# Pair 0 split from its two stacked q-k blocks, the weight clamp on GpSimd, and a contiguous tile for the middle 512 tokens

## The chip, the cores and the metric

The kernel runs on one core of a Trainium2 chip. The metric is the device time of one execution in microseconds. Before the change three runs gave 817.54, 816.72 and 815.52 us, so the median is 816.72 us. About 0.3% of that, 2.45 us, is what a measurement of this kernel can tell from no change.

## What is computed

Attention with hash buckets for 2 x 8 heads of 768 tokens and 64 dimensions, then two feed-forward blocks over the 1536 tokens of 512 values that it gives. Cut to what matters:

```python
q_bucket = sum(((q @ proj) > 0) * powers); k_bucket = sum(((k @ proj) > 0) * powers)
scores = where(q_bucket == k_bucket, (q @ k.T) / sqrt(64), -1e9)
attn = softmax(scores) @ v                      # -> x: 1536 x 512
xn = x / sqrt(mean(x * x) + 1e-6) * rms_g
y = silu(xn @ w_gate) * (xn @ w_val) @ w_out    # 512 -> 1536 -> 512
h = y @ moe2_w_in; g = where(h > 0, h, exp(min(h, 0)) - 1)
out = g @ moe2_w_out                            # 512 -> 2048 -> 512
```

The five weight matrices arrive as 64-bit floats and are turned into 32-bit ones on the chip.

## The kernel before

The work is written as some 2,700 tasks (`plan.add(engine, estimated us, function, reads, writes, ...)`) and the list `ORDER` says in which order their instructions are issued. There is no other scheduler: each engine takes its instructions in the order of that list and waits in front of the first one whose inputs or buffers aren't ready. All loads and stores go through SP's queue.

**Precision.** Every fp32 operand of a matmul is held as a high part rounded to `F32R` and a low part, the difference. A product is made of two or three passes (`PASS`: high x high, high x low, low x high).

**Attention.** Heads are worked in 8 pairs `j`, two heads `a` each. In memory `heads[2j+a]` holds three blocks of 128 x 768: `qk` (q in the upper 64 partitions, k in the lower), `kk` (k twice) and `qq` (q twice); `load_x` loads all three for both heads, six transfers of 384 KB. `prep` makes the operands: `ps_b` (bits of the buckets, from `qk`), `bitt`, `ps_c` (one-hot codes, with the table `wsel`, which `spread_table` copies from the loaded `wtmp`), and two operand tiles for each head, `tk` (`operand_k`, from `kk`: ScalarE the high part, GpSimd the low part) and `tq` (`operand_q`, from `qq`: GpSimd high and low, and a DMA `tq<-tq` that copies the high part to the lower partitions). For pair 0 these are done in two halves of 384 columns. Then come 12 score tiles a head pair: `ps_s` (4 matmuls), `nm` (row maximum, VectorE), `p` (exponential, ScalarE), transposes `ps_p`, their split into `pt` (ScalarE and VectorE, for some units ScalarE and GpSimd through `pf`), and `ps_v`. Two double banks hold `ps_s`, so the third score waits for the first exponential. `ps_w` are warm-up matmuls with no result.

**Weights.** `weights` loads a part of a matrix as `wraw`, takes the upper words' magnitude (`c1`, ScalarE, into `wf`), clamps it from below by `LEAST` (`c2`, VectorE, line 851), and puts sign, exponent and mantissa together with three integer operations (`c3`, `c4`, `c5`, VectorE, lines 857, 864, 871). ScalarE then rounds it to `whi` and GpSimd subtracts it to `wlo` (line 897). There are 54 such parts; six belong to the first feed-forward group and are done during attention. `wf` lives in the pool `h3` of 14 half-size tiles, as do the loaded head blocks.

**Feed-forward.** The first layer's 1536 inner columns are worked in five groups (3, 3, 2, 2, 2 tiles of 128), the second's in six. Group 0 takes the tokens in four blocks of 384, all later groups in three blocks of 512. A hidden tile `ps_h` is 12 matmuls (4 slices of 512 inputs, 3 passes). The inputs `xn` lie in one tile for each batch of 768 tokens, so the middle block of 512 tokens (512 to 1023) lies in two tiles, and `proj_mm` makes it in two parts of 256 columns, 24 matmuls.

The names that the change touches are `load_x` (312), `operand_k`, `operand_q`, `prep`, `score`, `weights` with its `c2`, `xsrc`, `xkeys`, `spread_table`, and `ORDER`.

Of the kernel before, what the change touches and what calls it, by code (L numbers as in the profile page):

```python
# [1278 lines left out]
```

## Time and profile before

| what | value |
|---|---|
| runs, us | 817.54, 816.72, 815.52 (median 816.72) |
| the profiled execution | 817.51 us |
| its span, first to last instruction | 815.4 us |
| mean granted TensorE clock | 0.996 of 2.4 GHz |
| busy, share of the span | PE 98%, VectorE 72%, ScalarE 50%, GpSimd 37% |

A matmul's end is modelled in these records, so a busy PE may still be waiting; the shares are means over stages with different limits. The program has a start of some 20 us, attention until about 250 us, the first feed-forward layer until about 565 us, and the second to the end.

### The profile page before, as it was taken

Reading aid. Unit: us, or ns where it says so; the run is one execution under the profiler, and the core shown is the slowest. Engines: PE = TensorE matmul, PEld = TensorE weight load, DVE = VectorE, ACT = ScalarE, POOL = GpSimd, SP = SyncE. Lnnn points to the kernel's source line nnn. Section 1 sums busy time; section 2 is a strip of 40 time slices with the busy share of each in tenths; the row PEclk is TensorE's granted clock in tenths of the full one; section 3 lists DMA queues with packets and bytes.
Section 4 is the critical chain, followed back from the end, with each engine's and each line's share of the span. In section 5 each row is a group of like instructions: output and inputs, shape, how many; then the busy total and the mean of one; then the engine's idle time right before and its main releaser. Section 6 shows DMA issues by size and latency. Waiting matters only on the chain.

```text
span 815.4 us, 11836 instructions
## 1 busy us (share of the span) xinstructions
PE 798.4 (98%) x4498; PEld 704.1 (86%) x4498; DVE 589.0 (72%) x914; ACT 411.0 (50%) x771; POOL 299.7 (37%) x255
## 2 busy tenths in 40 slices
PE   7999999989999999999999999999999999999998
PEld 6999798978999999988888888888888888888887
DVE  4898999999995873344546566878757777777676
ACT  4999898978995543322232232345544233432331
POOL 5889888879897020020111121111221021211110
PEclk8999999999999999999999999999999999999999
DMA  7638733551020023103012123122222201010004
GB/s 238 199 98 259 261 107 98 156 165 31 10 55 24 1 78 104 29 24 103 26 52 78 53 78 117 40 77 78 78 78 77 79 27 51 27 53 26 27 1 154
DMA packets 29592, 67.62 MB, mean 83 GB/s; under 512 B 3168, under 2 KB 3808, under 8 KB 29536
## 3 DMA queue, kind: packets, MB, share of 16 engines
q1 hardware_dynamic: 29536, 66.88, 26.4%
q8 instruction: 35, 0.57, 0.3%
q14 instruction: 21, 0.17, 0.1%
HBM read 57.82 MB, written 3.15 MB: 75 GB/s over the span
## 4 chain that ended last, share of the span: by engine, by line
PE 83%; DVE 9%; ACT 4%; issue 2%; DMA 1%; POOL 1%; SPq 0%; ACTq 0%; POOLq 0%
PE ps_h L946 40%; PE ps_o L1086 15%; PE ps_y L1031 12%; PE ps_s L514 5%; PE ps_p L559 5%; PE ps_v L606 4%; DVE nm L521 3%; DVE pt L571 2%; ACT p L531 1%; ACT pt L567 1%; DMA wtmp<-in_table_dram 1%; DMA vn<-in_v_dram 1%; PE ps_x L664 1%; DVE h L996 1%; DVE wf L851 0%
## 5 line engine op out<-in xcount | busy, mean ns | idle before, releaser
L897 POOL TENSOR_TENSOR wlo<-wf,whi 128x768 fp32r<-128x768 f32 (+1 forms) x54 | 92.4, 1724 | 446.1 <-ACT whi L893 379.3
L946 PE MATMUL ps_h<-xn,whi 128*128 128x256 f32 (+2 forms) x768 | 190.2, 336 | 0.0
L946 PEld LDWEIGHTS ps_h<-xn,whi 128*128 128x128 f32 x768 | 133.8, 189 | 11.9
L946 PE MATMUL ps_h<-xn,wlo 128*128 128x256 f32 (+2 forms) x384 | 128.9, 336 | 0.0
L992 ACT CAST h<-hf 128x512 fp32r<-128x512 f32 (+1 forms) x87 | 51.9, 606 | 134.2 <-DVE hf L986 47.0
L1086 PE MATMUL ps_o<-whi,h 128*128 128x512 f32 (+1 forms) x388 | 118.8, 387 | 0.4 <-DVE oa L1098 0.2
L946 PE MATMUL ps_h<-y,whi 128*128 128x512 f32 x384 | 118.2, 389 | 0.0
L521 DVE TENSOR_REDUCE nm<-ps_s 128x1 f32<-128x768 f32 x96 | 91.0, 948 | 6.1 <-PE ps_s L514 5.7
L606 PE MATMUL ps_v<-pt,vv 128*128 128x256 f32 x576 | 93.7, 292 | 0.6 <-DVE ot L624 0.2
L971 ACT ACTIVATE sg<-ps_h 128x512 f32<-128x512 f32 (+1 forms) x87 | 49.6, 580 | 87.4 <-PE ps_h L946 61.8
L514 PE MATMUL ps_s<-tk,tq 128*128 128x384 f32 x384 | 89.7, 356 | 2.9 <-ACT p L531 2.7
L1031 PE MATMUL ps_y<-h,whi 128*128 128x512 f32 (+1 forms) x312 | 91.7, 374 | 0.4 <-DVE h L996 0.4
L531 ACT ACTIVATE p<-ps_s,nm 128x768 f32<-128x768 f32 x96 | 87.2, 909 | 6.0 <-DVE nm L521 4.8
L559 PE MATMUL ps_p<-ident,p 128*128 128x128 f32 x576 | 84.3, 276 | 4.3 <-DVE pt L571 3.3
L1086 PEld LDWEIGHTS ps_o<-whi,h 128*128 128x128 f32 x388 | 72.6, 188 | 15.9 <-DVE oa L1098 0.7
L571 DVE TENSOR_TENSOR pt<-ps_p,pt 128x512 fp32r<-128x512 f32 x120 | 79.8, 681 | 8.7 <-ACT pt L567 7.6
L946 PEld LDWEIGHTS ps_h<-y,whi 128*128 128x128 f32 x384 | 72.1, 188 | 14.9
L996 DVE TENSOR_TENSOR h<-hf,h 128x512 fp32r<-128x512 f32 (+1 forms) x87 | 65.3, 762 | 23.9 <-ACT h L992 23.5
L606 PEld LDWEIGHTS ps_v<-pt,vv 128*128 128x128 f32 x576 | 78.7, 189 | 2.4 <-DVE pt L571 0.6
L946 PEld LDWEIGHTS ps_h<-xn,wlo 128*128 128x128 f32 x384 | 72.6, 189 | 5.7
L559 PEld LDWEIGHTS ps_p<-ident,p 128*128 128x128 f32 x576 | 67.4, 142 | 11.3 <-DVE pt L571 4.6
L567 ACT CAST pt<-ps_p 128x512 fp32r<-128x512 f32 x120 | 69.0, 587 | 12.8 <-PE ps_p L559 9.6
(89 smaller groups left out, 1287.2 us busy)
## 6 DMA issues: line engine op xcount, KB each, us to landing
wraw<-in_moe_w_out_dram SPq DMA_DIRECT2D x12, 768.0 KB, 4.5
qk<-in_heads_dram SPq DMA_DIRECT2D x16, 384.0 KB, 4.1
qq<-in_heads_dram SPq DMA_DIRECT2D x16, 384.0 KB, 4.0
kk<-in_heads_dram SPq DMA_DIRECT2D x16, 384.0 KB, 5.4
wraw<-in_moe_w_in_dram SPq DMA_DIRECT2D x8, 768.0 KB, 4.5
wraw<-in_moe_w_out_dram SPq DMA_DIRECT2D x10, 512.0 KB, 3.4
tq<-tq SPq DMA_DIRECT2D x21, 192.0 KB, 3.0
vn<-in_v_dram SPq DMA_DIRECT2D x8, 384.0 KB, 4.6
```

Source lines behind the costliest of these rows:

```text
L514: nc.tensor.matmul(st[B_][:, hf, 0:HS], lhsT=tq[:, x, c * 128:(c + 1) * 128], rhs=tk[:, x, hf * HS:(hf + 1) * HS], start=(x == 0), stop=(x ...
L521: nc.vector.tensor_reduce(out=st["nm", u, cc], in_=st[B_][:, :, 0:HS], axis=AX.XY, op=ALU.max, negate=True,)
L531: nc.scalar.activation(out=halves(st["p", u][:, cc]), in_=st.pop(B_)[:, :, 0:HS], func=AF.Exp, bias=st["nm", u, cc], scale=1.0, accum_out= ...
L559: nc.tensor.transpose(out=st[B_][:, o:o + 128], in_=p[:, cc, (2 * n + kt) * 128:(2 * n + kt + 1) * 128], identity=ident,)
L567: nc.scalar.copy(out=st[T_][:, 0], in_=st[B_])
L571: nc.vector.tensor_tensor(out=pt[:, 1], in0=st.pop(B_), in1=f(pt[:, 0]), op=ALU.subtract)
L606: nc.tensor.matmul(st[B_][:, 0:256], lhsT=st["vv", j][:, a, 2 * n + kt, :], rhs=pt[:, x, kt * 256:(kt + 1) * 256], start=(n == seq[0] and ...
L897: nc.gpsimd.tensor_tensor(out=l, in0=s["w"], in1=f(h), op=ALU.subtract)
L946: nc.tensor.matmul(ps[:, o:o + ln], lhsT=w[wp][:, kk, ft * 128:(ft + 1) * 128], rhs=t[xp][:, s:s + ln], start=(kk == 0 and n == 0), stop=( ...
L996: nc.vector.tensor_tensor(out=h[:, 1, 0:bw], in0=s["hf"], in1=f(h[:, 0, 0:bw]), op=ALU.subtract)
L1031: nc.tensor.matmul(s["ps"][:, 0:bw], lhsT=wo[wp][:, ft, m * 128:(m + 1) * 128], rhs=h[:, xp, 0:bw], start=(ft == 0 and i == 0), stop=(ft = ...
L1086: nc.tensor.matmul(s["ps"], lhsT=h[:, xp, t * 128:(t + 1) * 128], rhs=wo[wp][:, ft, ds], start=(ft == 0 and i == 0), stop=(ft == n - 1 and ...
```

## The change

Pair 0 loads only its two `qk` blocks. A new function, `first`, makes all its operands from them: ScalarE writes k and the scaled k into the two halves of `tk`, VectorE the low part of k and two scaled copies of q, GpSimd the high and the low part of q. The DMA `tq<-tq` is gone for pair 0, and the loads of pair 1 no longer wait for pair 0's first score. `spread_table` moves from VectorE to ScalarE. The clamp `c2` moves from VectorE to GpSimd, with a second bound that changes no weight. Sixteen new GpSimd copies (`middle`) put the middle 512 tokens into eight tiles of `h3`; `xsrc` hands these to groups 1 to 4 of the first layer. The list `ORDER` is a new one throughout. The estimates of `dma` differ, which by themselves issue nothing.

```diff
 def load_x(j, prio):
+        parts = ((0, 0), (0, 1)) if j == 0 else ((0, 0), (0, 1), (1, 0), (2, 0), (1, 1), (2, 1))
+        for n, (x, a) in enumerate(parts):
             dma(
-                lambda x=x, a=a: go(a, x), S * 128 * 4, r=[("go", j - 1)],
+                lambda x=x, a=a: go(a, x), S * 128 * 4, r=[("go", j - 1)] if j > 1 else [],
...
+    def first(a, prio):
...
+        def khi8():
+            nc.scalar.activation(out=operand(0, a, 1)[up, 0], in_=src()[dn], func=AF.Copy, scale=QSCALE)
+        def khi():
+            nc.scalar.copy(out=operand(0, a, 1)[dn, 0], in_=src()[dn])
+        def klo():
+            t = operand(0, a, 1)
+            nc.vector.tensor_tensor(out=t[dn, 1], in0=src()[dn], in1=f(t[dn, 0]), op=ALU.subtract)
+        def qhi8(x):
+            nc.vector.tensor_scalar(
+                out=operand(0, a, 0)[dn, x], in0=src()[up], scalar1=QSCALE, scalar2=None, op0=ALU.mult
+            )
+        def qhi():
+            nc.gpsimd.tensor_copy(out=operand(0, a, 0)[up, 0], in_=src()[up])
+        def qlo():
+            t = operand(0, a, 0)[up, 0]
+            nc.gpsimd.tensor_tensor(out=t, in0=src()[up], in1=f(t), op=ALU.subtract)
...
             def c2():
-                nc.vector.tensor_scalar(
-                    out=s["w"], in0=s["w"], scalar1=LEAST, scalar2=None, op0=ALU.max
+                nc.gpsimd.tensor_scalar(
+                    out=s["w"], in0=s["w"], scalar1=MOST, scalar2=LEAST, op0=ALU.min, op1=ALU.max
                 )
...
     def xsrc(g, blk, kk):
+        if li == 0 and g and blk == 1:
+            return [(0, st["mid", kk], 0, bw)]
...
+    def middle(prio):
+        def copy(kk, p, b):
+            if ("mid", kk) not in st:
+                st["mid", kk] = [half([128, 512], F32R, "mid") for _ in range(2)]
+            nc.gpsimd.tensor_copy(
+                out=st["mid", kk][p][:, b * 256:(b + 1) * 256],
+                in_=st["xn", b, kk][:, p, (1 - b) * 512:(1 - b) * 512 + 256],
+            )
...
     def spread_table():
-            nc.vector.tensor_copy(out=wsel[rows, hf], in_=st["wtmp"][rows])
+            nc.scalar.copy(out=wsel[rows, hf], in_=st["wtmp"][rows])
```

What the new list does at the places that the prediction speaks of:

SP's queue at the program's start, before (`qk`, `qq`, `kk`: head blocks; `pj`: the hash projection; `wtmp`: the table; `vn`: v):

```order
L321 DMA qk<-in_heads_dram 128x768
L1142 DMA pj<-in_proj_dram 128x32
L321 DMA qk<-in_heads_dram 128x768
L321 DMA qq<-in_heads_dram 128x768
L321 DMA kk<-in_heads_dram 128x768
L1135 DMA wtmp<-in_table_dram 128x256
L321 DMA kk<-in_heads_dram 128x768
L405 DMA tq<-tq 64x384
L332 DMA vn<-in_v_dram 128x768
```

SP's queue there, after:

```order
L322 DMA qk<-in_heads_dram 128x768 x2
L1207 DMA pj<-in_proj_dram 128x32
L1200 DMA wtmp<-in_table_dram 128x256
L322 DMA qk<-in_heads_dram 128x768 x2
L334 DMA vn<-in_v_dram 128x768
L322 DMA qq<-in_heads_dram 128x768
```

The table has two head blocks ahead of it in place of four, and what follows it are loads of pair 1 and v.

TensorE at the start, before:

```order
L1148 MATMUL ps_w<-ident 128x128 x11
L424 MATMUL ps_b<-qk,pj 32x384 x4
L1148 MATMUL ps_w<-ident 128x128 x5
L443 MATMUL ps_c<-bitt_82,wsel 128x384 x4
L514 MATMUL ps_s<-tk,tq 128x384 x12
L559 MATMUL ps_p<-ident,p 128x128 x4
L514 MATMUL ps_s<-tk,tq 128x384 x4
```

TensorE at the start, after:

```order
L1213 MATMUL ps_w<-ident 128x128 x10
L465 MATMUL ps_b<-qk,pj 32x384 x4
L1213 MATMUL ps_w<-ident 128x128 x3
L484 MATMUL ps_c<-bitt_82,wsel 128x384 x3
L1213 MATMUL ps_w<-ident 128x128 x3
L484 MATMUL ps_c<-bitt_82,wsel 128x384
L557 MATMUL ps_s<-tk,tq 128x384 x8
L465 MATMUL ps_b<-qk,pj 32x384 x4
L557 MATMUL ps_s<-tk,tq 128x384 x4
```

Three warm-up matmuls now stand between the third and the fourth `ps_c`, and pair 1's `ps_b` stands ahead of the third score.

VectorE at the first weight part (`wf_1077`), in pair 2, before:

```order
L624 TENSOR_TENSOR ot_1218<-ps_v_1129,ot_1218 64x256
L851 TENSOR_SCALAR wf_1077<-wf_1077 128x768
L521 TENSOR_REDUCE nm_1260<-ps_s_1220 128x1
L857 TENSOR_SCALAR wf_1077<-wf_1077 128x768
L571 TENSOR_TENSOR pt_1270<-ps_p_1225,pt_1270 128x512
L521 TENSOR_REDUCE nm_1285<-ps_s_1251 128x1
```

VectorE there, after (the part is `wf_1050`):

```order
L564 TENSOR_REDUCE nm_1217<-ps_s_1165 128x1
L900 TENSOR_SCALAR wf_1050<-wf_1050 128x768
L716 TENSOR_TENSOR xT_1163<-ot_763,ps_x_1204 128x384
L564 TENSOR_REDUCE nm_1240<-ps_s_1208 128x1
L667 TENSOR_TENSOR ot_1238<-ps_v_1113,ot_1238 64x256
L614 TENSOR_TENSOR pt_1247<-ps_p_1225,pt_1247 128x512
```

GpSimd there, after:

```order
L383 TENSOR_TENSOR tk_1034<-kk_886,tk_1034 64x768
L342 CAST vv_1072<-vn_955 128x6x64
L348 TENSOR_TENSOR vv_1072<-vn_955,vv_1072 128x6x64
L894 TENSOR_SCALAR wf_1050<-wf_1050 128x768
L623 CAST pt_1128<-pf_1090 128x512
L348 TENSOR_TENSOR vv_774<-vn_672,vv_774 128x6x64
```

The clamp has left VectorE's row and stands in GpSimd's between an operation on v and the cast of a transposed tile; VectorE's first operation on that part is now `c3` (line 900), which waits for it.

## Rows read from the trace of the kernel before

**Rows 1.** The page: busy time by engine, and the chain by engine.

```profile
PE 798.4 (98%) x4498; PEld 704.1 (86%) x4498; DVE 589.0 (72%) x914; ACT 411.0 (50%) x771; POOL 299.7 (37%) x255
...
PE 83%; DVE 9%; ACT 4%; issue 2%; DMA 1%; POOL 1%; SPq 0%; ACTq 0%; POOLq 0%
```

**Rows 2.** Windows: stretch, length, busy PE, PEld, DVE, ACT, POOL, clock, DMA share, GB/s.

```profile
12.00:20.00 8.00, 7.06 (x27) 6.07 (x26) 5.63 (x8) 5.98 (x13) 7.65 (x12) 0.57 0.82 280
20.00:80.00 60.00, 60.00 (x460) 56.82 (x458) 53.07 (x82) 58.24 (x120) 53.16 (x53) 1.00 0.61 184
80.00:160.00 80.00, 76.20 (x572) 71.05 (x570) 78.64 (x116) 72.72 (x146) 66.31 (x57) 1.00 0.54 164
160.00:240.00 80.00, 75.73 (x545) 68.37 (x544) 77.57 (x118) 69.34 (x143) 68.33 (x62) 1.00 0.21 57
```

**Rows 3.** Chain that ended last, the program's start: start us, us, what.

```profile
3.04 6.43 DMA wtmp<-in_table_dram
...
10.20 1.06 DVE wsel L1157
...
11.31 0.46 PE ps_c L443
...
12.78 0.68 PE ps_s L514 x2
...
14.48 1.00 ACT p L531 x2
...
20.57 0.78 PE ps_b L424 x8
21.35 0.90 PE ps_s L514 x4
```

**Rows 4.** DMA issues of the first microseconds: KB, us to landing.

```profile
qk<-in_heads_dram SPq DMA_DIRECT2D x1, 384.0 KB, 3.1
...
qq<-in_heads_dram SPq DMA_DIRECT2D x1, 384.0 KB, 6.1
```

**Rows 5.** Timeline of the start: start us, us, engine, line, operation.

```profile
0.72 0.38 SPq L321 DMA_DIRECT2D qk<-in_heads_dram  x1
...
7.12 1.38 PE L1148 MATMUL ps_w<-ident 128*128 128x128 f32 x10
```

**Rows 6.** Windows of TensorE alone: stretch, length, busy, clock, DMA share, GB/s.

```profile
13.00:17.00 4.00, 3.21 (x11) 0.52 0.73 235
```

**Rows 7.** Groups by shape: count, busy us, mean ns, idle before.

```profile
L851 DVE TENSOR_SCALAR wf<-wf 128x768 f32<-128x768 f32 x28 | 20.8, 747 | 8.3 <-ACT wf L848 8.3
...
L897 POOL TENSOR_TENSOR wlo<-wf,whi 128x768 fp32r<-128x768 f32 x28 | 55.7, 2003 | 245.5 <-ACT whi L893 212.4 <-PE ps_h L946 18.6 <-PE ps_o L1086 14.6
...
L409 POOL TENSOR_TENSOR tq<-qq,tq 64x768 fp32r<-64x768 f32 x14 | 26.8, 1917 | 0.5
...
L398 POOL TENSOR_SCALAR tq<-qq,share 128x768 fp32r<-128x768 f32 x14 | 14.2, 1012 | 2.0 <-DMA qq<-in_heads_dram 1.8
...
L893 ACT CAST whi<-wf 128x768 fp32r<-128x768 f32 x28 | 23.4, 839 | 12.4 <-DVE wf L871 12.4
```

**Rows 8.** The clamp, line 851: its durations until 260 us; VectorE's time from 80 to 245.

```profile
L851 DVE TENSOR_SCALAR wf<-wf x6: 544/1240/1545, 84.1 to 195.4; 128x768 f32<-128x768 f32 x6
...
80.00:245.00 165.00, 6.57 (x6) 1.00 0.38 112
```

**Rows 9.** Chain in the first layer: one middle and one outer hidden tile.

```profile
405.31 2.87 PE ps_h L946 x24
...
412.29 2.72 PE ps_h L946 x12
```

**Rows 10.** Chain in both layers: the longest pieces that aren't TensorE's.

```profile
503.36 2.70 DVE h L996 x2
...
673.90 1.51 DVE sg L980
...
767.37 1.66 DVE wf L851 x2
```

More of the change, by code (lines that the diff above doesn't have):

```diff
@@ L18 @@
 LEAST = 2.0 ** -15
+MOST = 3.4028234663852886e38
 SLOTS, H3S, PTS = 22, 14, 4
@@ L311, in dma @@
     def dma(fn, nbytes, r=(), w=(), prio=None):
-        return plan.add("SP", max(0.57, nbytes / 360e3), fn, r, w, prio, 2.7)
+        return plan.add("SP", max(0.5, nbytes / 315e3), fn, r, w, prio, 2.3)
     st = {}
@@ L321, in go @@
             nc.sync.dma_start(out=st["x", j, a, x], in_=heads[2 * j + a, x])
-        for n, (x, a) in enumerate(((0, 0), (0, 1), (1, 0), (2, 0), (1, 1), (2, 1))):
+        parts = ((0, 0), (0, 1)) if j == 0 else ((0, 0), (0, 1), (1, 0), (2, 0), (1, 1), (2, 1))
+        for n, (x, a) in enumerate(parts):
             dma(
-                lambda x=x, a=a: go(a, x), S * 128 * 4, r=[("go", j - 1)],
+                lambda x=x, a=a: go(a, x), S * 128 * 4, r=[("go", j - 1)] if j > 1 else [],
                 w=[("h3", "x", j, a, x)], prio=prio + 0.05 * n,
@@ L414, in operand_q, with src, key @@
         plan.add("Pool", pool(n), lo, [X_], los, prio)
+    def first(a, prio):
+        X_ = ("h3", "x", 0, a, 0)
+        def src():
+            return st["x", 0, a, 0]
+        def key(i, *parts):
+            return [okey(0, a, i, (x, h)) for x in parts for h in range(2)]
+        def khi8():
[14 more added lines that the diff above has]
+            nc.gpsimd.tensor_tensor(out=t, in0=src()[up], in1=f(t), op=ALU.subtract)
+        plan.add("ACT", act(S) + 0.12, khi, [X_], key(1, "hi"), prio)
+        plan.add("DVE", dve(S), klo, [X_, *key(1, "hi")], key(1, "lo"), prio)
+        plan.add("ACT", act(S) + 0.25, khi8, [X_], key(1, "up"), prio)
+        for x, part in enumerate(("hi", "dup")):
+            plan.add("DVE", 0.065 + S / 1920.0 + 0.2, lambda x=x: qhi8(x), [X_], key(0, part), prio)
+        plan.add("Pool", 0.83, qhi, [X_], key(0, "lo"), prio)
+        plan.add("Pool", pool(S), qlo, [X_], key(0, "lo"), prio)
     def prep_bits(j, prio):
@@ L491, in prep @@
         for a in range(2):
-            for cols in ((0,), (1,)) if j == 0 else ((0, 1),):
-                operand_k(j, a, cols, prio + off("opk", j) + a * off("opa", j))
-                operand_q(j, a, cols, prio + off("opq", j) + a * off("opa", j))
+            if j == 0:
+                first(a, prio + a)
+            else:
+                operand_k(j, a, (0, 1), prio + off("opk", j) + a * off("opa", j))
+                operand_q(j, a, (0, 1), prio + off("opq", j) + a * off("opa", j))
     def unit(u):
@@ L537, in score @@
         need = [okey(j, a, 0, (p, c // 3)) for p in ("hi", "lo", "dup", "hot")]
-        need += [okey(j, a, 1, (p, hf)) for hf in range(2) for p in ("hi", "lo", "hot")]
+        need += [okey(j, a, 1, (p, hf)) for hf in range(2) for p in ("hi", "lo", "hot", "up")]
         plan.add("PE", 4 * mm(HS) + 0.04, pe, need, w, prio + off("S", j))
@@ L877, in weights @@
             slow = 1.0
-            plan.add("DVE", slow * (0.065 + cols / 1920.0), c2, [], [W_], prio)
+            plan.add("Pool", 0.12 + cols * 0.00105, c2, [], [W_], prio)
             plan.add("DVE", slow * (0.065 + cols / 1920.0), c3, [], [W_], prio)
@@ L926, in xkeys @@
             return [(("slot", "y2", kk, p), x) for kk in range(KD) for p in range(2) for x in units(g, blk)]
+        if g and blk == 1:
+            return [(("h3", "mid", kk, p), b) for kk in range(KD) for p in range(2) for b in range(B)]
         keys = []
@@ L950, in proj_mm @@
             )
+    def middle(prio):
[6 more added lines that the diff above has]
+            )
+        for b in range(B):
+            for kk in range(KD):
+                for p in range(2):
+                    plan.add(
+                        "Pool", 0.36, lambda kk=kk, p=p, b=b: copy(kk, p, b),
+                        [(("slot", "xn", b, kk), p, 1 - b)],
+                        [(("h3", "mid", kk, p), b)] + ([(("h3", "mid", kk, 1), "got")] if p == 0 else []), prio,
+                    )
     def wkeys(g, m):
@@ L1156, in spread_table @@
             rows = slice(64 * hf, 64 * hf + 64)
-            nc.vector.tensor_copy(out=wsel[rows, hf], in_=st["wtmp"][rows])
-    plan.add("DVE", 0.55, spread_table, [("h3", "wtmp"), "wzero"], ["wsel"], -28)
+            nc.scalar.copy(out=wsel[rows, hf], in_=st["wtmp"][rows])
+    plan.add("ACT", 0.75, spread_table, [("h3", "wtmp"), "wzero"], ["wsel"], -28)
     load_v(0, -27)
@@ L1194 @@
     pos = float(NU)
+    middle(pos + 8)
     prev = None
```

276 rows, old and new, of the table ORDER are left out of this document.

## The prediction

> **What bounds the kernel now.** I read the page's busy shares and chain first, then windows by stage, then the chain of the start, and at last the groups by shape. TensorE is busy for 98% of the span and makes 83% of the chain; VectorE makes 9% [rows 1]. The windows say where these 9% lie. From 20 to 80 us TensorE is busy for all of 60.00 us, so what is gained ahead of 20 us is passed on. From 80 to 240 us it shows 151.9 of 160 us, while VectorE is busy for 156.2 of 160 us: there VectorE sets the pace, and TensorE lacks at least 8.1 us, more where a busy matmul is a waiting one [rows 2]. From about 240 us TensorE runs without a gap but for three places [rows 10]. Ahead of 20 us the chain is that of loading the table `wtmp`, which lands at 3.04 + 6.43 = 9.47 us, of copying it into `wsel` until 11.26, and of `ps_c` at 11.31; the first exponential starts at 14.48 and the fifth score at 21.35 [rows 3]. TensorE's granted clock was 0.52 of full speed, its lower level, from 13 to 17 us [rows 6], after it had stood from the end of the warm-up at 8.50 to 11.31 us [rows 3, 5].
>
> **The start.** Removed: four 384 KB loads of pair 0, its four `tq<-tq` copies, and the table's place behind four head blocks. SP's first issue is at 0.72 us [rows 5], the table's, the sixth, at 3.04 [rows 3], so issues are 0.46 us apart; as the fourth the table is issued at about 2.1. The first block took 3.1 us to land, the third 6.1 [rows 4]. So the table lands between 5.2 and 8.2; it has two blocks ahead of it and is a third of a block, and I take 6.6. The first `qk` lands at 3.8. From there three engines work side by side. ScalarE: the two high parts of k, by its cast of 768 columns 0.84 each [rows 7], until 5.5, then the table: the trace has no such copy on ScalarE; on VectorE the second took 1.06 [rows 3], as the upper bound for each, the lower is a third of a 768-column cast, 0.28; I take 0.4, nearer the cast, which is ScalarE's own, so `wsel` is ready at 6.6 + 0.8 = 7.4 (6.1 to 10.3). GpSimd: the high and the low part of q, 1.01 and 1.92 [rows 7], until 6.7. VectorE: two scaled copies of q, between the shortest and the longest clamp of that width, 0.54 and 1.55 [rows 8], the low part of k and the bits; these are ready between 7.4 and 8.7. So `ps_c` starts at 7.6 to 8.7, against 11.31: 2.6 to 3.7 us earlier. The three warm-up matmuls behind it cost 6 x 0.138 = 0.83 [rows 5], beside the one-hot copies that the score needs anyway. With 3.2 us the first exponential starts at 11.3. From there to the fifth score it was 6.87 us [rows 3]. Pair 1's `ps_b`, 0.78 [rows 3], now fills a wait: 0.8 less. If the clock stays up since TensorE no longer stands for 2.8 us, that stretch shrinks by up to two more microseconds; I don't count on it. **Sum 4.0 us**, bounds 1 (the table as late as 10) and 6. ScalarE, with 58.24 of 60 us busy from 20 to 80 [rows 2], is next in line there; its work behind the first exponential is not longer than before.
>
> **The clamp during attention.** Six clamps took VectorE 6.57 us between 80 and 245 us, 0.54 to 1.55 each [rows 8]. All of that stretch is VectorE's, so the gain has 6.6 us as its upper bound. The lower: a clamp of 1.2 us is one of 0.54 that waited, and where GpSimd was the cause, `c3`, now first, waits in its place; then 6 x 0.54 = 3.3 are left, and if TensorE finds something else to wait for, nothing. GpSimd's price for the two-bound form isn't in the trace; the nearest row is `tq<-qq,share`, two operations with immediate or column operands over 128x768: 1.01 [rows 7]; the upper bound is its subtraction, 1.92 to 2.00 [rows 7]. Six of these add 6 to 12 us to the 134.6 us that GpSimd works from 80 to 240 [rows 2]; it has 25 idle. `c3` waits for GpSimd on VectorE, and behind it in that row stand a maximum, a join and a subtraction for which ScalarE and TensorE wait; the order leaves one or more of GpSimd's operations between. **Sum 3.5 us**, bounds -2 and 6.6.
>
> **The middle tile.** A middle hidden tile of 24 matmuls takes 2.87 us, an outer one of 12 takes 2.72 [rows 9]. Groups 1 to 4 have 9 column tiles, each for gate and value: 18 x 0.15 = **2.7 us**, in a stage where TensorE never waits. The sixteen copies of 256 columns cost GpSimd about a third of 1.01 each, 5.4 us in all, in a stage where it stands idle for hundreds of microseconds ahead of `wlo` [rows 7]; they are needed only at group 1's second block. Were that cover gone, the price is 5.4 us once. The Trainium skill, "TensorE: Matmul & The Clock Gate", section "Back-to-back issue gap", gives a lone matmul N / 2.4 + 2.5 ns at full clock; by that 216 matmuls fewer would save an estimated 0.5 us. The rows give 0.15 us for 12 matmuls, 12.5 ns each; I go by them.
>
> **The clamp in the feed-forward layers.** 48 clamps leave VectorE, which gains nothing where TensorE sets the pace, but for the two that made a piece of 1.66 us of the chain [rows 10]. The same 48 add to GpSimd some 22 x 1.01 and 26 x 0.7 (that form scaled to 512 columns), 40 us. Two other pieces, 2.70 for two subtractions and 1.51 for one operation [rows 10], are VectorE's stretched; more GpSimd work makes more of these. I set the gain against the loss: **0**, bounds -3 and +1.7. Eight of the 14 tiles of `h3` go to the middle tokens through the first layer; 48 parts in some 550 us need one or two at a time, so six are enough, at no cost.
>
> **Sum.** 4.0 + 3.5 + 2.7 + 0 = 10.2 us. The profiled execution took 817.51 us (its span 815.4 and 2.1 around it), so 807.3; the median of the runs stands 0.8 below the profiled one, so I forecast **806.5 us**.
>
> **Rivals.** (1) *VectorE's time goes to other waits.* For it: the clamps' spread, 0.54 to 1.55 [rows 8], shows that VectorE's operations are held up by something beside them, and GpSimd gets busier. The attention term falls to 0 and the feed-forward stage loses 1: 811.0. The Trainium skill, "SBUF — State Buffer", section "Who interferes with whom", says that VectorE and GpSimd share a port pair which one of them holds for a whole instruction while the other is blocked; it speaks for this rival, and the clamps' spread agrees with it. (2) *Slower: the clamp as a wait in order.* `c3` heads VectorE's row until GpSimd has done the clamp, which may itself stand behind a `wlo` of 2.00 us [rows 7]; VectorE's sums and subtractions, which free TensorE's banks, stand behind it. It decides from 10.2 / 48 = 0.21 us of TensorE's time for each feed-forward part; at 0.3 us the time is 806.5 + 14.4 = 821. For it: one stretched operation of 1.5 us did reach TensorE. Against it: 54 `wlo`s ran beside VectorE, and three places in over 500 us lost anything [rows 10]. (3) *The table is late again*, 6.4 us after its issue as before, with ScalarE's copies at 1.06: the start gives 1 in place of 4: 809.5. For it: every transfer behind the first took 6 us or more until 10 us [rows 3, 4]. Against it: fewer bytes ahead. (4) *All terms at their good ends*, the clock staying up: 6 + 6.6 + 2.7 + 0 = 15.3: 801.4. (5) *The 0.15 us belong to that place and not to the number of matmuls*: the middle term falls to 0, 809.2; the other middle tiles of the chain with the same 2.87 us speak against it [rows 9]. The skill's formula above speaks for it. That the change doesn't do what it says can't be for the matmuls, whose order has none of 256 columns left in `ps_h`.
>
> **How the numbers follow.** Forecast 0.50, (1) 0.16, (2) 0.05, (3) 0.12, (4) 0.15, (5) 0.02. A measurement of this kernel can tell about 0.3%, 2.45 us, from no change. Faster by more than that: all but (2) and those parts of (1) and (3) where both go wrong together, 0.07: 0.88. Within: 0.07. Slower: 0.05. The range: (2), and the 0.07 near no change, are left out above, and some 0.06 of (4) below: 801 to 812.5.
>
> **What would show it.** Right: `ps_c` at 8 us or so and the first exponential at about 11; the first layer's middle hidden tiles at 2.72 us as the others; VectorE still nearly full from 76 to 235 us but without line 851; the first feed-forward matmul some 7 us earlier than before; about 1 us for a clamp on GpSimd. Wrong: `ps_c` at 10 or later; a clamp of 2 us on GpSimd; VectorE waiting for GpSimd ahead of `c3`; more than the three old places on the chain behind 270 us. The forecast fails as a whole if the new order makes attention's units meet in another way than before, with waits of TensorE between 20 and 80 us, where there were none.

## The result, and the profile after

The changed kernel took 808.41 us (median of four runs, 807.17 to 809.12), against 816.22 us for the kernel before beside it: a ratio of 0.990, 95% interval 0.988 to 0.992. It is faster by some 8 us; forecast were 806.5 us and 801 to 812.5. Measured again later, beside the variants, it took 807.18 us against 815.89 (ratio 0.988, 0.9865 to 0.990). The profiled execution took 808.29 us with a span of 806.5, which is 8.9 us less than before, where the sum had 10.2; the second measurement (e5) has a span of 805.5, 9.9 us less.

The page of the changed kernel, busy time and chain, answers to [rows 1]: VectorE has lost 13 us of work, GpSimd gained 48, and VectorE's share of the chain has not shrunk.

```profile
PE 793.1 (98%) x4282; PEld 690.9 (86%) x4282; DVE 576.0 (71%) x864; ACT 414.8 (51%) x776; POOL 347.4 (43%) x317
...
PE 82%; DVE 11%; ACT 2%; issue 2%; POOL 1%; DMA 1%; ACTq 0%; SPq 0%; DVEq 0%; POOLq 0%
```

The windows of [rows 2] (stretch, length, busy PE, PEld, DVE, ACT, POOL, clock, DMA share, GB/s):

```profile
12.00:20.00 8.00, 7.25 (x51) 5.79 (x50) 7.81 (x11) 7.38 (x16) 4.94 (x6) 1.00 0.27 76
20.00:80.00 60.00, 59.76 (x453) 57.20 (x454) 53.97 (x82) 57.52 (x118) 52.77 (x54) 1.00 0.57 183
80.00:160.00 80.00, 79.14 (x596) 73.55 (x595) 77.68 (x120) 74.93 (x153) 73.49 (x64) 1.00 0.47 148
160.00:240.00 80.00, 75.96 (x531) 69.36 (x530) 75.82 (x110) 68.52 (x140) 68.43 (x64) 0.98 0.25 70
```

From 12 to 20 us VectorE is now the full engine (7.81 of 8 us, before 5.63) and the clock stays at its upper level (1.00, before 0.57). From 80 to 160 us TensorE is busy for 79.14 us (before 76.20). From 160 to 240 us little is won.

The chain at the start (start us, us, what), beside [rows 3], is no longer that of the table: from 3.86 us to 22.15 it is VectorE's alone:

```profile
3.86 1.65 DVE tq L438 x2
...
5.86 2.14 DVE tk L435
...
8.03 0.63 DVE bitt L471
...
8.79 0.60 PE ps_c L484 x2
...
10.01 0.61 DVE tq L438
...
18.66 1.29 DVE tk L435
```

In the timeline of the same stretch (start us, us, engine, line, operation) stand the table's two copies, the first exponential and the fifth score:

```profile
6.06 0.82 ACT L1222 CAST wsel<-wtmp 64x256 fp32r<-64x256 f32 x2 [0.50 <-DMA wtmp<-in_table_dram]
...
12.55 0.90 ACT L574 ACTIVATE p<-ps_s,nm 128x768 f32<-128x768 f32 x1 [0.82 <-DVE nm L564]
...
16.66 0.97 PE L557 MATMUL ps_s<-tk,tq 128*128 128x384 f32 x4
```

The table is ready at 6.88, but the bucket bits only at 8.66, because VectorE's low part of k (line 435) took 2.14 us. The first exponential is 1.9 us earlier than before, the fifth score 4.7.

How much of this reaches TensorE is read from the number of its matmuls started by 70 us. Before (scores `ps_s`, products with v `ps_v`, one-hot codes `ps_c`; stretch, length, busy us, count, clock, DMA share, GB/s):

```profile
0.00:70.00 70.00, 26.44 (x108) 0.95 0.61 192
0.00:70.00 70.00, 21.09 (x128) 0.95 0.61 192
0.00:70.00 70.00, 4.02 (x12) 0.95 0.61 192
```

The same three after:

```profile
0.00:70.00 70.00, 26.44 (x116) 1.00 0.52 169
0.00:70.00 70.00, 22.43 (x136) 1.00 0.52 169
0.00:70.00 70.00, 4.86 (x15) 1.00 0.52 169
```

and what they cost in the chain of the changed kernel:

```profile
192.69 0.47 PE ps_v L649 x4
193.16 0.18 PE ps_c L484
...
195.52 0.70 PE ps_s L557 x4
```

Transposes stand at 144 in both. So at 70 us the changed kernel is ahead by 8 x 0.175 + 8 x 0.118 + 3 x 0.18 = 2.9 us: that is the start's worth, where the sum had 4.0. The same count gives 3.1 in e5 (116, 138, 15) and 2.4 in e9 (114, 136, 14), whose code is the same up to there. And some of it may be the clock of the one execution it is read against: before's profile has a mean granted clock of 0.996, with 0.57 from 12 to 20 us [rows 2]. Of the 41 executions of before beside the variants, the 13 with a mean clock of 1.000 took 815.4 us in the mean, the 18 with 0.997 or less 817.0; where in the program the clock fell in these, no trace shows.

The rest is in one table, from the first matmul of `ps_h`, the first of `ps_o` and the end of the span; attention, the first and the second layer are three lengths that add up to it, each read from the one execution that was profiled. The variants are those of the next section; e1 to e8 ran on one chip, e9 to e11 on a second, e12 on a third, so ratios, each to before beside it, compare better than medians.

| kernel | median us | ratio to before, 95% | attention ends | first layer | second layer |
|---|---|---|---|---|---|
| before | 816.22 | | 241.7 | 324.5 | 249.2 |
| changed | 808.41 | 0.988 to 0.992 | 235.6 | 321.3 | 249.6 |
| changed, again (e5) | 807.18 | 0.9865 to 0.990 | 234.1 | 321.4 | 250.0 |
| e1 middle in two | 808.51 | 0.989 to 0.992 | 234.3 | 324.3 | 249.4 |
| e2 clamp on VectorE | 814.30 | 0.9965 to 0.998 | 242.0 | 321.3 | 249.9 |
| e3 clamp on GpSimd in attention alone | 807.09 | 0.986 to 0.991 | 233.0 | 321.3 | 250.0 |
| e4 no clamp | 807.69 | 0.987 to 0.991 | 234.4 | 321.4 | 249.5 |
| e6 before, clamp on GpSimd | 811.77 | 0.993 to 0.996 | 237.4 | 324.2 | 248.6 |
| e7 no low q of head 0 | 807.21 | 0.987 to 0.9905 | 233.4 | 321.4 | 249.6 |
| e8 low k early | 807.43 | 0.987 to 0.991 | 234.5 | 321.4 | 249.4 |
| e9 join moved | 805.28 | 0.985 to 0.988 | 232.4 | 321.4 | 249.8 |
| e10 four loads back | 808.33 | 0.987 to 0.992 | 237.0 | 321.3 | 250.0 |
| e11 low q on VectorE | 804.53 | 0.984 to 0.988 | 234.8 | 321.3 | 249.5 |
| e12 e9 and e11 | 804.37 | 0.984 to 0.987 | 232.6 | 321.3 | 249.6 |

The layers repeat within some 0.6 us from program to program with the tile; attention scatters by 1 to 3 us between executions of code that is the same up to there (the changed kernel, e1, e3 and e5: 233.0 to 235.6). A difference of 1 us in a median is therefore read in its stage or not at all.

### The profile page after: what moved, and what is told of

Its sections match the earlier page's. It is cut to its first block, busy times and chain, and to the rows that moved or that the text cites. A ratio compares the mean times of both kernels' runs of the same rounds, so it can differ in the third digit from the quotient of the medians.

```text
span 806.5 us, 11405 instructions
## 1 busy us (share of the span) xinstructions
PE 793.1 (98%) x4282; PEld 690.9 (86%) x4282; DVE 576.0 (71%) x864; ACT 414.8 (51%) x776; POOL 347.4 (43%) x317
## 3 DMA queue, kind: packets, MB, share of 16 engines
q1 hardware_dynamic: 28640, 64.91, 25.3%
## 4 chain that ended last, share of the span: by engine, by line
PE 82%; DVE 11%; ACT 2%; issue 2%; POOL 1%; DMA 1%; ACTq 0%; SPq 0%; DVEq 0%; POOLq 0%
PE ps_h L993 38%; PE ps_o L1151 16%; PE ps_y L1096 12%; PE ps_v L649 5%; PE ps_p L602 5%; PE ps_s L557 4%; DVE nm L564 3%; DVE pt L614 2%; DVE wf L907 1%; DVE h L1061 1%; ACT p L574 1%; ACT pt L610 1%; DVE wf L914 1%; PE ps_c L484 1%; DVE wf L900 1%
## 5 line engine op out<-in xcount | busy, mean ns | idle before, releaser
L940 POOL TENSOR_TENSOR wlo<-wf,whi 128x768 fp32r<-128x768 f32 (+1 forms) x54 | 90.7, 1687 | 187.8 <-ACT whi L936 171.7
L993 PE MATMUL ps_h<-xn,whi 128*128 128x512 f32 (+1 forms) x480 | 138.3, 369 | 0.0
L894 POOL TENSOR_SCALAR wf<-wf 128x768 f32<-128x768 f32 (+1 forms) x54 | 45.5, 848 | 198.7 <-ACT wf L891 198.2
L993 PEld LDWEIGHTS ps_h<-xn,whi 128*128 128x128 f32 x480 | 88.4, 188 | 11.7
L1061 DVE TENSOR_TENSOR h<-hf,h 128x512 fp32r<-128x512 f32 (+1 forms) x87 | 68.7, 806 | 34.9 <-ACT h L1057 34.7
L557 PE MATMUL ps_s<-tk,tq 128*128 128x384 f32 x384 | 87.9, 350 | 1.5 <-ACT p L574 1.0
L993 PE MATMUL ps_h<-xn,wlo 128*128 128x512 f32 (+1 forms) x240 | 88.2, 367 | 0.0
L602 PE MATMUL ps_p<-ident,p 128*128 128x128 f32 x576 | 82.5, 276 | 1.9 <-DVE pt L614 0.8
L1151 PE MATMUL ps_o<-wlo,h 128*128 128x512 f32 (+1 forms) x194 | 75.1, 387 | 0.0
L993 PE MATMUL ps_h<-y,wlo 128*128 128x512 f32 x192 | 74.7, 389 | 0.0
```

What stands on the lines that cost most here:

```text
L557: nc.tensor.matmul(st[B_][:, hf, 0:HS], lhsT=tq[:, x, c * 128:(c + 1) * 128], rhs=tk[:, x, hf * HS:(hf + 1) * HS], start=(x == 0), stop=(x ...
L602: nc.tensor.transpose(out=st[B_][:, o:o + 128], in_=p[:, cc, (2 * n + kt) * 128:(2 * n + kt + 1) * 128], identity=ident,)
L940: nc.gpsimd.tensor_tensor(out=l, in0=s["w"], in1=f(h), op=ALU.subtract)
L993: nc.tensor.matmul(ps[:, o:o + ln], lhsT=w[wp][:, kk, ft * 128:(ft + 1) * 128], rhs=t[xp][:, s:s + ln], start=(kk == 0 and n == 0), stop=( ...
L1061: nc.vector.tensor_tensor(out=h[:, 1, 0:bw], in0=s["hf"], in1=f(h[:, 0, 0:bw]), op=ALU.subtract)
L1151: nc.tensor.matmul(s["ps"], lhsT=h[:, xp, t * 128:(t + 1) * 128], rhs=wo[wp][:, ft, ds], start=(ft == 0 and i == 0), stop=(ft == n - 1 and ...
```

## The experiments

**The middle tile undone (e1).**

```diff
     def xsrc(g, blk, kk):
-        if li == 0 and g and blk == 1:
-            return [(0, st["mid", kk], 0, bw)]
     def xkeys(g, blk):
-        if g and blk == 1:
-            return [(("h3", "mid", kk, p), b) ...]
```

> The changed kernel (808.4 us) with one thing undone: groups 1 to 4 of the first layer read the middle 512 tokens from the two batch tiles again, in two parts of 256 columns; the sixteen GpSimd copies stay, unread. If the 0.15 us of a middle hidden tile belongs to the number of its matmuls, the 18 middle tiles take 2.87 us in place of 2.72 and the time is 808.4 + 2.7 = 811.1 us (810.4 to 811.8), with the first layer, from the first hidden tile to the first output tile, 2.7 us longer. If it belongs to the place, or a matmul's own price is the 2.5 ns of the page (216 of them, an estimate of 0.5 us), the time is 808.4 to 808.9 us and the middle tiles stay at 2.72 us.

The median, 808.51 us, seemed to say that the tile is worth nothing. The stages say otherwise: the first layer took 324.3 us against 321.3 or 321.4 in every kernel that has the tile. Chain of this variant, and of the changed kernel, one middle tile each:

```profile
392.79 2.87 PE ps_h L989 x24
```

```profile
393.19 2.72 PE ps_h L993 x12
```

So 216 more matmuls cost 3.0 us, 14 ns each, and the price belongs to their number. The profiled executions differ by 809.81 - 807.26 = 2.55 us (e1 and e5), the medians by 1.3: the rest is scatter of attention and of the second layer. The clock is part of why the first comparison misled: all executions of e1 and of e5 had a mean granted clock of 1.000, the four of the changed kernel's first measurement 0.998 or 0.999.

**The changed kernel again (e5)**, with no edit.

> The changed kernel itself, unaltered, beside the next ones on one chip. The first four variants showed attention ending between 233.0 and 235.6 us (first feed-forward matmul) in programs that are the same up to there, so part of every difference of 1 to 3 us is attention's own scatter. If that scatter is by chance, the time is 808.4 us within 1, attention ends between 233 and 236 us, and the kernel with the middle in two parts (808.5 us) was lucky in its attention. If the middle tile is worth nothing after all, this run is at 808.4 us with the same attention as that one (234.3 us) and the same first layer (324.3 us).

807.18 us and attention's end at 234.1 in place of 235.6, with the same code: the scatter is there without any edit. The reading "worth nothing" falls with the first layer's length, 321.4 here and 324.3 in e1.

**The clamp back on VectorE (e2), and off it in the old order (e6).**

```diff
-                nc.gpsimd.tensor_scalar(
-                    out=s["w"], in0=s["w"], scalar1=MOST, scalar2=LEAST, op0=ALU.min, op1=ALU.max
+                nc.vector.tensor_scalar(
+                    out=s["w"], in0=s["w"], scalar1=LEAST, scalar2=None, op0=ALU.max
```

> The changed kernel with all 54 clamps back on VectorE in their old one-bound form, each at the same place of the order. By my sum (VectorE sets the pace of attention from 80 to 235 us, and the feed-forward layers don't care): six clamps come back on VectorE, the first feed-forward matmul is 3.5 to 4.5 us later than 235.7, the rest stays as long as it is, total 812 to 813 us. By rival 1 (VectorE's time goes to other waits): first feed-forward matmul within 1 us of 235.7, total 808 to 809.5 us. By rival 2 (VectorE's waits for GpSimd's clamp cost TensorE time in the feed-forward layers): the feed-forward layers, from the first hidden tile to the end, get 1 to 3 us shorter than 570.8 us.

e6 is the reverse edit in the kernel before.

> The kernel before with one part of the change: all 54 clamps on GpSimd in the two-bound form, in the old order. Putting the clamps back on VectorE in the changed kernel made attention 6.4 us longer (first feed-forward matmul 242.0 against 235.6 us). If a clamp on VectorE costs attention that much whatever the order, this kernel is 5 to 6.5 us faster than before, 810 to 811.4 us, with the first feed-forward matmul at 235.5 to 237 us. By my sum, 3.5 us: 812.9 us, 238.2 us. If the two orders were each made for their own clamp, so that either misplaced one costs waits (rival 1, or rival 2 in attention): within 1.5 us of before, 815 to 818 us, with VectorE waiting for GpSimd ahead of the first integer operation.

In the new order the clamp's return cost 814.30 - 807.18 = 7.1 us, all of it in attention (242.0 against 234.1 or 235.6); in the old order its removal gave 4.1 us, attention 4.3. VectorE's time shows why. Groups of VectorE from 70 to 235 us, first with the clamp on VectorE (e2; count, busy us, mean ns, idle before; line 894 is the clamp, 900, 907 and 914 the integer operations):

```profile
L914 DVE SCALAR_TENSOR_TENSOR wf<-wraw,wf 128x768 int32<-128x768 int32 x5 | 7.8, 1556 | 0.0
...
L907 DVE SCALAR_TENSOR_TENSOR wf<-wraw,wf 128x768 int32<-128x768 int32 x6 | 7.1, 1184 | 0.0
L894 DVE TENSOR_SCALAR wf<-wf 128x768 f32<-128x768 f32 x6 | 6.5, 1084 | 0.1
L900 DVE TENSOR_SCALAR wf<-wf 128x768 int32<-128x768 int32 x6 | 6.3, 1068 | 0.0
```

then the changed kernel (e5):

```profile
L914 DVE SCALAR_TENSOR_TENSOR wf<-wraw,wf 128x768 int32<-128x768 int32 x5 | 8.4, 1686 | 0.0
L907 DVE SCALAR_TENSOR_TENSOR wf<-wraw,wf 128x768 int32<-128x768 int32 x6 | 7.6, 1275 | 0.0
...
L900 DVE TENSOR_SCALAR wf<-wf 128x768 int32<-128x768 int32 x6 | 4.6, 779 | 0.0
```

27.7 against 20.6 us: 7.1 us of VectorE, 7.9 of attention. In the old order the four lines took 25.3 us before and 20.1 with the clamp gone: 5.2 of VectorE, 4.3 of attention. There the first integer operation grew from 6.3 to 7.8 us, so it did inherit some of the clamp's waiting; in the new order it did not. VectorE's time in attention is TensorE's time, nearly one for one. The 7.1 us are not the clamp's worth alone: with the clamp on VectorE the new order ends attention at 242.0 us, the old one at 241.7, though the start is 2.9 us ahead. So some of it is the price of an order that was made for a clamp elsewhere, and the 4.1 us of the old order are the cleaner figure.

**The 48 clamps of the feed-forward layers (e3), and all of them (e4).**

```diff
+                if g == 0:
                     nc.gpsimd.tensor_scalar(...)
+                else:
+                    nc.vector.tensor_scalar(out=s["w"], in0=s["w"], scalar1=LEAST, ...)
```

> The changed kernel with the clamps of the first feed-forward group (the six during attention) on GpSimd and the other 48 back on VectorE, same order. Attention must be as in the changed kernel, first feed-forward matmul at 235.7 us within 0.5. By my sum (the 48 clamps are worth nothing on either engine): 808.4 us within 0.7. By rival 2 (waiting for GpSimd ahead of the first integer operation, 13.6 us of waits in 7 places, reaches TensorE): 1 to 3 us faster, 805.5 to 807.4 us. If instead clamps on VectorE stall TensorE more, as before the change at three places (2.9 us together): 809.5 to 811 us.

> The changed kernel without any clamp: its 54 operations are left out, on both engines (weights below the least one come out wrong), all else in the same order. It bounds what the clamp still costs where it is. By my sum, in which GpSimd's clamp lies wholly beside other work: 807.5 to 808.4 us, and the first feed-forward matmul at 235 to 235.7 us. By rival 2, or if GpSimd's clamps stretch VectorE's operations beside them: 804 to 807 us, with the places at 299, 681 and 754 us gone from the chain.

e3: 807.09 us, the two layers 571.3 us together, e5 571.4. e4: 807.69 us, 570.9. In the feed-forward layers the clamp is worth nothing on either engine, and leaving it out gives 0.5 us there at most, which is no more than their scatter. The waits that rival 2 needs are there all the same, in the changed kernel (the clamp's durations; then who waited for it, us and times):

```profile
L894 POOL TENSOR_SCALAR wf<-wf x54: 609/830/1421, 72.5 to 757.7; 128x768 f32<-128x768 f32 x28, 128x512 f32<-128x512 f32 x26
...
  DVE wf L900: 13.6, 7
```

**The start: what stretches the low part of k (e7, e8).** e7 leaves GpSimd's subtraction for the first head out; e8 puts VectorE's ahead of it.

```diff
         def qlo():
+            if a:
                 nc.gpsimd.tensor_tensor(out=t, in0=src()[up], in1=f(t), op=ALU.subtract)
```

> The changed kernel without GpSimd's subtraction for the low part of q of the very first head (5.18 to 7.18 us); that one operation is left out, so this head's low part of q is wrong. Theory: VectorE's low part of k beside it took 2.14 us because the two engines' two-input operations keep each other out; without GpSimd's the same instruction takes 0.95 to 1.0 us, the bucket bits start at 6.9 in place of 8.03, the first one-hot matmul at 7.6 in place of 8.79 and the first exponential at about 11.4 in place of 12.55; total about 1 us less, 807.4 us. Rival: the instruction is slow by itself there (its operands lie in the lower partitions, or its input has just been written): it stays at 2.1 us, and so do the starts behind it.

```diff
 VectorE's row at the start
 L438 TENSOR_SCALAR tq<-qk 64x768
-L438 TENSOR_SCALAR tq<-qk 64x768
-L1191, L1193 MEMSET share
 L435 TENSOR_TENSOR tk<-qk,tk 64x768
+L438 TENSOR_SCALAR tq<-qk 64x768
 L471 TENSOR_SCALAR bitt<-ps_b,floor 128x384
 L497 TENSOR_SCALAR tq<-ps_c 64x384
+L1191, L1193 MEMSET share
```

> The changed kernel with another order on VectorE at the start and nothing else: the low part of k of the first head straight behind ScalarE's high part, between the two scaled copies of q, so that it runs before GpSimd's subtraction; the bucket bits ahead of the three fills of the column table. Theory (the start is VectorE's chain, and the low part of k is stretched by GpSimd's subtraction): low part of k in 1.0 us from 4.7, bits at about 6.3, first one-hot matmul at 7.0 to 7.3 when the table is copied (6.9), first exponential 1 to 1.5 us earlier than 12.55; total 0.8 to 1.5 us less, 807 to 807.6 us. Rival (the table or ScalarE is next in line): first one-hot matmul at 8 us or later, total within 0.4 us of the changed kernel.

VectorE's timeline without the subtraction (e7):

```profile
5.77 0.95 DVE L435 TENSOR_TENSOR tk<-qk,tk 64x768 fp32r<-64x768 f32 x1
```

and with the other row (e8), where GpSimd's subtraction runs as before:

```profile
4.64 1.19 DVE L435 TENSOR_TENSOR tk<-qk,tk 64x768 fp32r<-64x768 f32 x1 [0.31 <-ACT tk L431]
5.84 2.08 DVE L438 TENSOR_SCALAR tq<-qk 64x768 fp32r<-64x768 f32 x1
```

Without it 0.95 us in place of 2.14: the theory holds. With it the instruction that then stands there pays, 2.08 us in place of the 1.17 that the second copy takes in the changed kernel (the first takes 0.55), and the bits start at 7.95 as in e5 (7.97): a new wait took the old one's place. The Trainium skill, "SBUF — State Buffer", section "Who interferes with whom", says that VectorE and GpSimd share one pair of ports, that a VectorE operation with two SBUF inputs contends with a GpSimd instruction that reads SBUF, that a copy or scalar operation in a two-port mode contends with GpSimd too, and that one engine then blocks for the other's whole instruction. The trace agrees: both kinds waited here, and `pt` (line 614), with one input from PSUM, took 632 to 693 ns each of its 120 times in the changed kernel. Whether the copy of q runs in such a mode, no run here shows.

Of e7's gain, 0.9 us at the first exponential, 0.7 was left at attention's end (233.4 against 234.1 in e5), and nothing can be told in the median.

**The four loads issued again (e10).**

```diff
     def ld_table():
+        more(0)      # qq and kk of head 0, read by nobody
         st["wtmp"] = half([128, 2, 128], F32, "wtmp")
         nc.sync.dma_start(out=st["wtmp"], in_=table)
+        more(1)
```

> The changed kernel with pair 0's four dropped loads (two of them ahead of the table, two behind it, as before the change) issued again into buffers that nobody reads; all engines' work is otherwise that of the changed kernel. If the start's gain is the table's (rival 3 turned on by hand): the table lands at 8 to 9.5 us in place of 6.0, its copies on ScalarE end at about 10, the first one-hot matmul is at 10 to 10.5 in place of 8.73, the first exponential 1.3 to 2 us later than 12.43, total 808.5 to 809.5 us. If VectorE's chain hides most of the table's lateness, because it is only ready at 8.6 anyway: first exponential at most 0.7 us later, total within 0.8 us of 807.2. A third case: pair 1's blocks, now behind four more loads, come late for the fifth score at 19.85 us, and more than 2 us are lost, over 809.5 us.

Timeline of this variant, the table's copies, then from its chain the load for the operand of pair 1:

```profile
8.36 0.82 ACT L1228 CAST wsel<-wtmp 64x256 fp32r<-64x256 f32 x2 [2.96 <-DMA wtmp<-in_table_dram]
...
7.94 7.17 DMA kk<-in_heads_dram
```

The table's copies start 2.4 us later than in e5 (5.96), the first exponential only 0.5 (12.96 against 12.43), since VectorE's bits end at about 8.5 anyway. But pair 1's `kk` block landed at 15.1 and is now on the chain, and by the counts at 70 us (112 scores, 132 `ps_v`, 13 `ps_c`) 1.5 of the start's 2.9 us are gone. Total 808.33 us, 1.1 more than e5, with intervals that overlap: between the first two cases, by a piece of the third. (The score at 19.85 us that the expectation calls the fifth is the seventh in e5; its fifth starts at 16.55.) What the dropped loads give is an early pair 1 besides an early table; how the 1.5 us divide between the two was not tried.

**The join at 177 us (e9).** In attention's second half stands an instruction that no term of the sum had. VectorE in the changed kernel:

```profile
177.03 3.72 DVE L914 SCALAR_TENSOR_TENSOR wf<-wraw,wf 128x768 int32<-128x768 int32 x1
```

GpSimd beside it:

```profile
176.88 1.27 POOL L626 TENSOR_TENSOR pt<-pf,pt 128x512 fp32r<-128x512 f32 x1
178.12 1.81 POOL L738 TENSOR_TENSOR sq<-sq 128x768 f32<-128x768 f32 x1
180.02 1.42 POOL L894 TENSOR_SCALAR wf<-wf 128x768 f32<-128x768 f32 x1
```

The join spans both subtractions and ends 0.8 us after the second, which ends at 179.93; the clamp behind takes 1.42 in place of 0.83. TensorE waits behind it, for the sum `ot` that is VectorE's next operation; the row maximum behind the bucket bits comes at 184.16:

```profile
181.13 0.73 PE L649 MATMUL ps_v<-pt,vv 128*128 128x256 f32 x4 [2.19 <-DVE ot L667]
...
184.16 0.95 DVE L564 TENSOR_REDUCE nm<-ps_s 128x1 f32<-128x768 f32 x1
```

In e3 the same place reads, VectorE and GpSimd,

```profile
177.33 1.99 DVE L919 SCALAR_TENSOR_TENSOR wf<-wraw,wf 128x768 int32<-128x768 int32 x1
```

```profile
178.41 2.59 POOL L738 TENSOR_TENSOR sq<-sq 128x768 f32<-128x768 f32 x1
```

Here the join got in between the two, and the second paid. The edit moves it behind the bucket bits:

```diff
 VectorE's row at that place
 L614 TENSOR_TENSOR pt<-ps_p,pt 128x512
-L914 SCALAR_TENSOR_TENSOR wf<-wraw,wf 128x768
 L667 TENSOR_TENSOR ot<-ps_v,ot 64x256 x2
...
 L471 TENSOR_SCALAR bitt_83<-ps_b,floor 128x384
+L914 SCALAR_TENSOR_TENSOR wf<-wraw,wf 128x768
```

> The changed kernel with one VectorE instruction moved: the second integer join (line 914) of the weight part that is worked at 177 us stands five instructions later, behind the next bucket bits, where GpSimd had nothing to do. In the changed kernel it took 3.72 us there (0.94 to 1.1 us elsewhere), from the start of GpSimd's two-input operations until these made room, TensorE lacked some 2.2 us and its granted clock was 0.50 for the two microseconds behind. Theory (that stretch is on TensorE's path): the instruction takes 0.95 to 1.3 us, first feed-forward matmul 2 to 3 us earlier than 234.1 to 235.6 us, total 1.5 to 3 us less than 807.2 (the changed kernel on this chip), 804.2 to 805.7 us. Rival (VectorE is late by as much anyway, or the stretch goes to the next instruction in the row): total within 0.8 us of 807.2.

VectorE in that variant:

```profile
181.28 0.95 DVE L914 SCALAR_TENSOR_TENSOR wf<-wraw,wf 128x768 int32<-128x768 int32 x1
```

805.28 us, attention's end at 232.4 (234.1 and 235.6 in the changed kernel): the stretch was on TensorE's path. From the start of GpSimd's `pt` to the row maximum behind the bits it is 7.28 us in the changed kernel, both times, and 5.30 in e9:

```profile
182.15 0.95 DVE L564 TENSOR_REDUCE nm<-ps_s 128x1 f32<-128x768 f32 x1
```

So the join's place is worth 2.0 us. The totals say 1.5 (ratio 0.9864 against 0.9882), with intervals that overlap.

The same place accounts for most of attention's scatter. The join took 3.71 to 3.73 us in the changed kernel, e1, e5, e7, e8, e10 and e11. From its start to attention's end it is 57.4 us in e1, e5, e7 and e8, where the clock stayed at 1.00 behind it; 58.2 to 58.6 in the changed kernel's first profile, e10 and e11, where it fell to its lower level; and 55.7 in e3, where the join took 1.99.

**The first head's low part of q on VectorE (e11), and both (e12).**

```diff
         def qlo():
-            nc.gpsimd.tensor_tensor(out=t, in0=src()[up], in1=f(t), op=ALU.subtract)
+            eng = nc.gpsimd if a else nc.vector
+            eng.tensor_tensor(out=t, in0=src()[up], in1=f(t), op=ALU.subtract)
```

> The changed kernel with another start: the first head's low part of q on VectorE in place of GpSimd (0.95 against 2.0 us), VectorE's row being copy of q, low part of k, low part of q, bits, second copy of q, and the three fills behind. Moving the low part of k ahead of GpSimd's subtraction gave nothing, since the copy that then stood beside it took 2.08 in place of 0.55 us; leaving the subtraction out made the start 0.9 us shorter. Theory (whatever VectorE does beside GpSimd's two-input operation waits for it, so take that operation out of the row): both low parts at 0.95 us, bits at 6.6, first one-hot matmul at 7.3 to 7.6, first exponential at 11.0 to 11.4 in place of 12.43; first feed-forward matmul 0.9 to 1.4 us earlier, total 805.9 to 806.6 us. Rival (the start's gain is eaten by the next waits in attention, as it was where the subtraction was left out: 807.2 us): total within 0.5 us of 807.2.

> The changed kernel with both moves that helped: the start with the first head's low part of q on VectorE (804.5 us alone, first exponential at 11.72 us) and the stretched integer join moved behind the bucket bits (805.3 us alone, first feed-forward matmul at 232.4 us). If the two are independent, and each is worth what its stage showed (0.7 us at the start's end, 1.7 us or more at 177 us): 803 to 804.2 us with the first feed-forward matmul at 231 to 232 us and no join over 1.6 us during attention. If moving the program's phase by the start's 0.7 us lets other two-input operations meet, as chance has it: 804.5 to 806 us, with another instruction of VectorE stretched beyond 2 us between 80 and 235 us.

e11's first exponential:

```profile
11.72 0.90 ACT L575 ACTIVATE p<-ps_s,nm 128x768 f32<-128x768 f32 x1 [0.67 <-DVE nm L565]
```

That is 0.7 us earlier than e5's, less than expected; by its counts at 70 us (116 scores, 142 `ps_v`, 16 `ps_c`) the start is worth 3.8 us in place of 2.9 (3.1 in e5). At the join of 176 us it is 0.5 us ahead of e5. The median is 804.53 us, 2.7 below e5's; its profiled execution, 807.37, was its slowest, with the clock at 0.50 from 182 to 184 us, so where the other executions gained the rest no trace shows. e12 took 804.37 us. The joins in attention took up to 1.72 us, where none over 1.6 was expected, and attention ended at 232.6, as in e9 alone: the start's 0.7 us did not add up. It was lost at 74 us, where TensorE waits for a DMA copy as it does not in e11:

```profile
75.35 0.59 PE L558 MATMUL ps_s<-tk,tq 128*128 128x384 f32 x2 [1.15 <-DMA tq<-tq]
```

A join that e11 starts at 89.87 us starts at 90.76 in e12. e12 is the fastest of these kernels, 0.9855 of before (0.984 to 0.987), though its interval still overlaps that of the changed kernel's second measurement (0.9865 to 0.990).

## Why the prediction came out as it did

**Sign, size and mechanism** held: 8.9 us in the span (9.9 in e5) where the sum had 10.2. The size is in part luck. The terms measured by themselves, 2.9 + 4.3 + 3.0, add up to 10.2 again, because the start's 1.1 too little and the 0.8 and 0.3 too much in the other two cancel; the 0.3 to 1.3 us that are then missing are left to the rest of the new order, which the sum had at nothing, and to scatter. By its steps:

- **Start, 4.0: measured 2.9.** The terms for the transfers and ScalarE were about right (table ready at 6.88, forecast 7.4; 0.41 a copy, forecast 0.4). For the low part of k and the bits the prediction named no price, so its bounds of 7.4 and 8.7 can't be worked out again. The failed step is "three engines work side by side": VectorE and GpSimd didn't, as e7 showed. VectorE's 2.14 us for the low part of k put the bits at the upper end of the bound (8.66 of 7.4 to 8.7), `ps_c` at 8.79 where the sum took 8.1, and another 0.6 us went between it and the first exponential, where a scaled copy of q (0.61 us at 10.01) now stands in VectorE's row: that came at 12.55 instead of 11.3. That the clock would stay up, which was not counted on, came true (1.00 from 12 to 20 us) and the fifth score came 4.7 us earlier (16.66 against 21.35), more than the sum's 4.0. But "what is gained ahead of 20 us is passed on" failed too: VectorE is the chain until 22 us, its second low part of k at 18.66 included, and 2.9 us were left at 70 us.
- **Clamp in attention, 3.5: 4.3 in the old order (e6), 6.4 to 7.9 in the new (e2).** The mechanism was right, the size too low: I had the next integer operation inherit all waiting, and it inherited 1.5 us or none. The upper bound of 6.6 was the clamp's own time; the new order's 6.4 to 7.9 hold some of its own price, as said at e2.
- **Missing from the sum: the new order's own price.** The join at 177 us took back 2.0 us (e9). The prediction looked at one place of the new order in attention, ahead of `c3`; the loss was at another instruction of the same weights.
- **Middle tile, 2.7: 3.0** (e1). The estimate of 0.5 us by the formula of the Trainium skill, "TensorE: Matmul & The Clock Gate", section "Back-to-back issue gap", falls: of the 24 matmuls' 2.87 us each takes 120 ns, 13 more than 256 columns at 2.4 GHz.
- **Clamp in the feed-forward layers, 0: 0** (e3, e4). The second layer is 0.2 to 0.8 us longer than before, with the clamp on either engine or none; that goes with the new order (with the clamp on GpSimd in the old one it is 248.6), and which place in it was not tried.
- **From the profiled time to the median.** I took 0.8 us off because the profiled execution of before lay above its median. That of the changed kernel lay 0.1 below its own. Of the 1.9 us between forecast and median, 1.0 is the sum's (807.3 against the profiled 808.29) and 0.9 this step's.

**Rivals.** (1), VectorE's time going to other waits, falls by e2 and e6. (2): its waits came (13.6 us, seven times), its price didn't (e3). (3), turned on by hand in e10, costs 1.1 us of total, not 3. (4) had the clock right and the start wrong. (5) falls by e1.

**Signs.** As said: middle tiles at 2.72 us, a clamp of 0.83 us in the median (about 1), VectorE nearly full without its clamp, the first feed-forward matmul 6.1 to 7.6 us earlier (some 7). Not as said: `ps_c` at 8.79 (8 or so) and the first exponential at 12.55 (about 11). Two signs of failure came without the failure: the waits ahead of `c3`, and more places behind 270 us than the three of [rows 10]. The chain of the changed kernel there has, among others,

```profile
306.34 2.20 DVE h L1061
...
682.83 1.70 DVE h L1061 x2
...
691.19 2.01 DVE sg L1045
...
754.07 2.56 DVE h L1061 x2
```

They are long VectorE operations again, at other places. Without the middle tile's 3.0 us the two layers would be 0.2 us longer than before (0.7 in e5), so these places cost little more than the old ones.

## What to carry to other kernels

Two engines that are both free are not two engines if their operations keep each other out: price an operation at its stretched duration where the other engine's row has two-input work beside it, and ask of a reordering which instruction will stand there next. Where one engine sets the pace of a stage, its saved time comes through nearly whole. Read an edit of 1 to 3 us in the length of its own stage, since the median of the whole may hide it.
